# Agent attention with a squared-ReLU feed-forward layer: casting every high half by DMA, and squaring every fifth block on VectorE

## The chip, the cores and the metric

The kernel runs on one core of a Trainium2 chip. The metric is the device time of one execution in microseconds (us); the median over runs is compared.

## The reference, cut to what matters

```python
def sm(a, b):
    s = scale * (a @ b.transpose(0, 2, 1))
    e = np.exp(s - s.max(-1, keepdims=True))
    return e / (e.sum(-1, keepdims=True) + 1e-09)
agent_v = sm(agents, k) @ v          # 4 batches, 12480 keys, 49 agents, 128 channels
x = sm(q, agents) @ agent_v          # 4 x 12480 queries
h = x.reshape(49920, 128) @ w_in     # 128 x 2048
r = np.maximum(h, 0.0)
out = (r * r) @ w_out                # 2048 x 128
```

All inputs are float32.

## The kernel before, in words

**The work.** The 49920 tokens are cut into 52 groups of 960 (two halves of 480 columns), the 2048 hidden units into 16 slices of 128. A pair of group and slice is a block; blocks are numbered i = 0 to 831, 16 to a group. `agent_v @ w_in` is multiplied out once for a batch (`w_make`), so that a block begins with the softmax weights of its group (49 rows for each half, kept as `p_a` and `p_b`).

**Two-part numbers.** A matmul on rounded float32 (fp32r) loses the low bits. So each operand is split into a high half (a cast to fp32r) and a low half (the value minus the high one), and a product is made of three matmuls: high with high, high with low, low with high.

**A block's path.** `mm1` (L401): six matmuls into a PSUM tile h, of which there are two. `relu` (L413) and `square` (L417), both on ScalarE, write g. `high` (L420) casts g to gh: for even blocks, and for all of the first 48, by a DMA that GpSimd issues (L423); otherwise by a copy on VectorE (L425); the last four blocks always take VectorE. `low` (L427) subtracts on VectorE and gives gl. `mm2` (L431) makes twelve matmuls of a block, six for each half, that add up in a PSUM pair `out` over the 16 blocks of a group. The two row halves of TensorE work side by side on the two banks of the pair, and for each pair of blocks the banks change sides once; between the sides a nop on GpSimd (L442, the relay) must pass. There are 10 buffers of g, 9 of gh and 7 of gl.

**The order.** One list holds every step with a time in units of blocks; each engine does its steps in the order of these times. Block i has `mm1` at i, `relu` at i + 0.1, `square` at i + 1.2, `high` at i + 3.05 (DMA) or i + 2.35, `low` at i + 5.2 (DMA) or i + 4.3. `mm2` follows LAG = 8 steps behind: an even block j with j + 1, one side at step j + 8, the other at j + 9. The times order the engines' queues; when a step runs is decided by its waits.

**The output.** After a group's last `mm2` ScalarE copies one half of `out` to ob and VectorE the other (`store_a` L458, `store_d` L462), and SP stores ob (L477). SP also issues all loads of queries, keys and values (six buffers in all, shared) and the four small transfers of `q_spread` (L374), in one queue.

**The attention part** is put between the blocks by a planner (`chain`, L504), which gives each step of a chain of engines the first free place in the list and keeps the PSUM pair that the insertion uses free of others (`held`, L522): `plan_queries` (L538) for two groups at a time, `plan_keys` and `plan_bias` for the next batch's keys, `plan_values` for exp, the turn of the weights (`k_turn`, tile pe), `v_acc` and, at its end, `a_final` and four `w_make`. `q_hi` (L383) casts a group's softmax weights by a GpSimd DMA to `p_a`, `q_lo` (L387) makes `p_b` on VectorE. Before the first block the keys and values of batch 0 are worked through in an order written by hand (from L602).

Of the kernel before, what the change touches and what calls it, by code (L numbers as in the profile page):

```python
# [17 lines left out]
P = 128  # L18
# [9 lines left out]
def agent_attention_relu2_kernel(ctx: ExitStack, tc: tile.TileContext, qT, kT, v, agT, w_in, w_out, outT):  # L28
# [354 lines left out]
    def q_hi(s):  # L383
        PT[s] = (wk.tile([P, TT], F32R, name="p_a"), wk.tile([P, TT], F32R, name="p_b"))
        nc.gpsimd.dma_start(out=PT[s][0][:M], in_=pts[s][:M])

# [30 lines left out]
    def square(i):  # L417
        nc.scalar.activation(gs[i], gs[i], AF.Square)  # L418

# [10 lines left out]

    def mm2(i, turn, first=False, last=False):  # L431

        s, j = divmod(i, NF)
        gh, gl = ghs[i], gls[i]
        if first:
            group[0] = s
            o = pair(s, "out")
            outs[s] = [o[:, t] for t in range(2)]
        o = outs[s]
        relay = None  # L440
        if turn != seen["turn"] and not first:
            relay = nc.gpsimd.nop()  # L442
            tc.add_manual_dep(relay.ins, seen["mm"].ins.name, SYNC, reason="bank changes row tile")
        for n, (w, g) in enumerate(((wo_hi, gh), (wo_lo, gh), (wo_hi, gl))):
            for t, rows in enumerate((LOW, HIGH)):
                u = t ^ turn
                mm = nc.tensor.matmul(o[u][:, :TT], w[rows, j, :], two(g[rows, u, :]), start=first and n == 0, stop=last and n == 2)  # L447
# [3 lines left out]
        done[i] = done.get(i, 0) + 1  # L451
        if done[i] == 2:
            ghs.pop(i), gls.pop(i)

    done = {}
    obs = {}

    def store_a(s):  # L458
        nc.scalar.copy(ob_of(s)[:, 0, :], outs[s][0][:, :TT])  # L459
        store(s)  # L460

    def store_d(s):  # L462
        nc.vector.tensor_copy(ob_of(s)[:, 1, :], outs[s][1][:, :TT])  # L463
        store(s)

    def ob_of(s):
        if s not in obs:
            obs[s] = wk.tile([P, 2, TT], F32, name="ob", bufs=1)
        return obs[s]

    def store(s):
        stored[s] = stored.get(s, 0) + 1
        if stored[s] == 2:
            ob = obs.pop(s)
            outs.pop(s)
            if s < NSG - 1:
                nc.sync.dma_start(out=outT[:, s * ST:(s + 1) * ST], in_=ob.rearrange("p t n -> p (t n)"))  # L477
            else:
                for t in range(2):
                    nc.sync.dma_start(out=outT[:, s * ST + t * TT:s * ST + (t + 1) * TT], in_=ob[:, t, :])  # L480

    stored = {}

    LAG = 8
    TAIL = 36
    SKIP = (7, 12)
    FROM = 0

    def by_dma(i):
        return FROM <= i < NG - 4 and (i % 2 == 0 or i < 3 * NF)  # L490

    steps = []

    def at(t, f, *args):
# [43 lines left out]
    def plan_queries(u):  # L538

        first, t = chain(32 * u - 46, [("PE", q_scores, u), ("DVE", q_turn, u)])  # L540
        for x, s in enumerate(members(u)):
            at(first - LEAD + .1 * x, q_load, s)
        plan_rows(u, t + 2)

    def plan_rows(u, g):
        todo = [("DVE", q_max, u), ("DVE", q_sub, u), ("ACT", q_exp, u), ("DVE", q_total, u), ("DVE", q_norm, u), ("DVE", q_back, u)]
        for e, f, _ in todo:
            _, t = chain(g, [(e, f, u)])
            g = t + 2
        at(t + .9, q_spread, u)  # L550
        plan_halves(u, t + 6)

    def plan_halves(u, t):
        for s in members(u):
            _, t = chain(max(t, s * NF - 9 if s > 1 else 0), [("POOL", q_hi, s), ("DVE", q_lo, s)])
            assert t + 1 < s * NF, (s, t)

    def plan_keys(b, n, t):

        first, end = chain(t, [("PE", k_scores, b, n), ("ACT", k_copy, n), ("DVE", k_max, n)])  # L560
        for x in range(2):
            if b > 1 or n > 1:
                at(first - LEAD + .1 * x, k_load, b, 2 * n + x)
        return end

# [4 lines left out]
    def plan_values(b, t0, stop):  # L570

        used = {}
        d = (stop - TAIL - t0) / NP
        for n in range(NP):
            _, t1 = chain(max(t0 + 1 + int(n * d), used.get(n - 2, 0)), [("ACT", k_exp, n), ("DVE", k_turn, n)])
            used[n], end = chain(t1 + 3, [("PE", v_acc, n), ("DVE", v_sum, n)])
            for x in range(2):
                at(used[n] - LEAD + .1 * x, v_load, b, 2 * n + x)
            if b < B - 1:
                keys = plan_keys(b + 1, n, t1 + 6)  # L580
        last, end = chain(end + 2, [("PE", a_final, 0), ("DVE", a_final, 1), ("DVE", a_final, 2)])
        for f in range(F // 512):
            _, end = chain(max(end + 2, stop + 4 * f - 12), [("PE", w_make, b, f, 0), ("PX", w_make, b, f, 1), ("ACT", w_make, b, f, 2), ("DVE", w_make, b, f, 3)])
            assert end + 2 < stop + 4 * f, (b, f, end, stop)
        if b < B - 1:
            return max(last + 2, plan_bias(keys + 1))

# [76 lines left out]
    for n, t in ((0, (.6, .61, .62, 1.15, 1.2, 1.3)), (1, (3.2, 3.21, 3.3, 3.6, 3.7, 3.8)), (2, (9.1, 9.11, 9.3, 10.1, 10.3, 11.1)), (3, (12.1, 12.12, 12.3, 13.1, 13.3, 14.1))):  # L664
        convert(wo_make, n, [y - Z for y in t])
        at(t[5] + .1, wo_split, n, 0)
        at(t[5] + 2.1, wo_split, n, 1)
    for t in (1.45, 2.45, 4.45, 5.45):
# [9 lines left out]
    taken.update((("ACT", 5), ("DVE", 6), ("ACT", 7), ("DVE", 8)))  # L678
    plan_halves(1, 11)
    for f, t in ((2, 5), (3, 7)):  # L680
        for x, y in enumerate((.005, .02, .5, 1.4)):
            at(t + y, w_make, 0, f, x)
    for u in range(2, NSG // 2 + 1):
        plan_queries(u)
    end = 22
    for n in range(NP):
# [5 lines left out]
    for i in range(NG):  # L692
        late = i in SKIP or i < NF + LAG and (i < LAG or (i - LAG) % NF == 0)
        at(i if late else i + .01, mm1, i)
        at(i + .1, relu, i)
        at(i + 1.2, square, i)
        if by_dma(i):
            at(i + 3.05, high, i)
            at(i + 5.2, low, i)
        else:  # L700
            at(i + 2.35, high, i)
            at(i + 4.3, low, i)
    for i in range(NF + LAG):
        j = i - LAG + sum(i <= x for x in SKIP)
        if j >= 0 and i not in SKIP:
            for x in range(2):
                at(i + (.03 if x else .005 if j == 0 else 0), mm2, j, x ^ (j % 2), x == 0 and j == 0, x == 1 and j == NF - 1)
    for j in range(NF, NG - LAG, 2):
        for x in range(2):
            for y in range(2):  # L710
                at(j + LAG + x + .001 * y, mm2, j + y, x ^ (j // 2 % 2), x + y + j % NF == 0, x + y == 2 and j % NF == NF - 2)
    for s in range(NSG - 1):
        t = s * NF + NF - 1 + LAG
        at(t + (.003 if s else .031), store_a, s)
        at(t + (.004 if s else .032), store_d, s)
    t, way = NG, (NG - LAG) // 2 % 2
    for js in (range(NG - LAG, NG - LAG // 2), range(NG - LAG // 2, NG)):
        for x in range(2):
            for j in js:
                at(t, mm2, j, way ^ x, False, x == 1 and j == NG - 1)  # L720
                t += 1
        way ^= 1
    at(t + .1, store_a, NSG - 1)
    at(t + .2, store_d, NSG - 1)
    with tc.manual_schedule():
# [32 lines left out]
```

## Time and profile before

| | us |
|---|---|
| median of 3 runs | 1781.02 |
| lowest and highest run | 1777.61, 1786.03 |
| the profiled execution's own time | 1783.28 |
| its span, first to last instruction | 1781.5 |
| TensorE busy in it (matmul) | 1736.2 |
| ScalarE busy | 1606.2 |
| VectorE busy | 1457.4 |
| GpSimd busy | 283.7 |

The profile is of one execution on the chip. Busy time is the time in which an engine works on an instruction; waits, register work and the issuing of a DMA by SP are not counted. The ends of matmuls are modelled, so TensorE's busy time says little alone. A wait is put down to what came last by the profile.

### The profile page before, as it was taken

Reading aid. Unit: us, or ns where it says so; the run is one execution under the profiler, and the core shown is the slowest. Engines: PE = TensorE matmul, PEld = TensorE weight load, DVE = VectorE, ACT = ScalarE, POOL = GpSimd, SP = SyncE. Lnnn points to the kernel's source line nnn. Section 1 sums busy time; section 2 is a strip of 40 time slices with the busy share of each in tenths; the row PEclk is TensorE's granted clock in tenths of the full one; section 3 lists DMA queues with packets and bytes.
Section 4 is the critical chain, followed back from the end, with each engine's and each line's share of the span. In section 5 each row is a group of like instructions: output and inputs, shape, how many; then the busy total and the mean of one; then the engine's idle time right before and its main releaser. Section 6 shows DMA issues by size and latency. Waiting matters only on the chain.

```text
span 1781.5 us, 41424 instructions
## 1 busy us (share of the span) xinstructions
PE 1736.2 (97%) x16841; PEld 1496.3 (84%) x16841; DVE 1457.4 (82%) x1740; ACT 1606.2 (90%) x1853; POOL 283.7 (16%) x509
## 2 busy tenths in 40 slices
PE   7899999999999999999999999999999999999998
PEld 3577888887888889887888889888988988988898
DVE  5876888878878888977878978888886887888887
ACT  3688989998889999999899999999998999999997
POOL 0232111111111111111111111111111111111110
PEclk8999999999999999999999999999999999999999
DMA  9689566666456567467356455456545545555553
GB/s 369 234 302 343 185 208 229 201 229 201 151 177 196 183 213 239 142 215 234 130 177 224 149 199 193 158 190 204 168 159 161 181 159 186 182 166 172 172 172 111
DMA packets 113791, 350.13 MB, mean 197 GB/s; under 512 B 15628, under 2 KB 28416, under 8 KB 113600
## 3 DMA queue, kind: packets, MB, share of 16 engines
q0 software_dynamic: 71264, 227.90, 37.4%
q1 hardware_dynamic: 42336, 119.59, 21.0%
q8 instruction: 132, 2.16, 0.5%
q14 instruction: 59, 0.48, 0.1%
HBM read 81.47 MB, written 25.56 MB: 60 GB/s over the span
## 4 chain that ended last, share of the span: by engine, by line
PE 80%; DMA 9%; DVE 4%; issue 3%; ACT 3%; POOL 0%; POOLq 0%; DVEq 0%; ACTq 0%
PE out L447 48%; PE h L411 24%; DMA gh<-g 9%; PE ps_att L167 4%; PE ps_att L230 2%; DVE gl L429 2%; ACT g L418 2%; ACT g L415 1%; PE out L230 1%; PE ps_att L310 1%; PE out L597 0%; DMA p_a<-pt 0%; DMA pt<-et 0%; DVE mxs L185 0%; DVE gh L425 0%
## 5 line engine op out<-in xcount | busy, mean ns | idle before, releaser
L429 DVE TENSOR_TENSOR gl<-g,gh 128x960 fp32r<-128x960 f32 x832 | 922.6, 1148 | 139.4 <-DMA gh<-g 134.5
L415 ACT ACTIVATE g<-h 128x960 f32<-128x960 f32 x832 | 820.1, 986 | 125.2 <-PE h L411 124.6
L418 ACT ACTIVATE g<-g 128x960 f32<-128x960 f32 x832 | 845.6, 1016 | 0.0
L447 PE MATMUL out<-gh,wo_hi 64*128 64x480 f32 x3328 | 623.4, 371 | 5.3 <-POOLq L442 3.1
L447 PE MATMUL out<-gl,wo_hi 64*128 64x480 f32 x3328 | 613.3, 365 | 7.3 <-DVE gl L429 6.9
L447 PE MATMUL out<-gh,wo_lo 64*128 64x480 f32 x3328 | 609.4, 363 | 0.0
L423 POOL DMA_DIRECT2D gh<-g x438 | 245.2, 560 | 1404.8 <-ACT g L418 482.9
L447 PEld LDWEIGHTS out<-gh,wo_hi 64*128 64x128 f32 x3328 | 314.0, 185 | 72.9 <-issue 38.9
L447 PEld LDWEIGHTS out<-gl,wo_hi 64*128 64x128 f32 x3328 | 314.5, 186 | 42.2 <-DVE gl L429 18.5
L447 PEld LDWEIGHTS out<-gh,wo_lo 64*128 64x128 f32 x3328 | 317.2, 187 | 22.0
L411 PE MATMUL h<-p_a,w_a 49*128 49x480 f32 x1664 | 310.9, 370 | 0.4 <-ACT w_a L294 0.4
L411 PE MATMUL h<-p_b,w_a 49*128 49x480 f32 x1664 | 304.2, 362 | 1.0 <-DVE p_b L388 1.0
L411 PE MATMUL h<-p_a,w_b 49*128 49x480 f32 x1664 | 304.6, 363 | 0.0
L425 DVE CAST gh<-g 128x960 fp32r<-128x960 f32 x394 | 257.0, 652 | 3.1 <-ACT g L418 3.0
L411 PEld LDWEIGHTS h<-p_a,w_a 49*128 49x128 f32 x1664 | 158.3, 187 | 16.4 <-ACT g L415 1.4
L411 PEld LDWEIGHTS h<-p_b,w_a 49*128 49x128 f32 x1664 | 159.8, 189 | 12.5 <-DVE p_b L388 1.4
L411 PEld LDWEIGHTS h<-p_a,w_b 49*128 49x128 f32 x1664 | 156.4, 184 | 13.0
L463 DVE COPY ob<-out 128x480 f32<-128x480 f32 x52 | 34.2, 658 | 108.1 <-ACT ob L459 108.1
L344 DVE STREAM_TRANSPOSE e<-ps_att 128x960 f32<-128x960 f32 (+1 forms) x26 | 30.7, 1182 | 34.9 <-PE ps_att L167 34.9
L167 PE MATMUL ps_att<-qt,ag_sb 128*32 128x480 f32 x408 | 47.3, 572 | 0.0
L209 ACT ACTIVATE sk<-sk,mb 128x448 f32<-128x448 f32 x56 | 33.9, 665 | 8.6 <-DVE mb L205 8.6
L230 PE MATMUL ps_att<-vt,pe 128*49 128x129 f32 x588 | 36.7, 275 | 2.1 <-DVE mxs L185 1.6
(92 smaller groups left out, 624.9 us busy)
## 6 DMA issues: line engine op xcount, KB each, us to landing
gh<-g POOLq DMA_DIRECT2D x438, 480.0 KB, 3.2
vt<-v SPq DMA_DIRECT2D x56, 451.5 KB, 9.3
kt<-kT SPq DMA_DIRECT2D x56, 448.0 KB, 6.6
qt<-qT SPq DMA_DIRECT2D x52, 480.0 KB, 7.2
outT<-ob SPq DMA_DIRECT2D x51, 480.0 KB, 3.5
pt<-et SPq DMA_DIRECT2D x204, 60.0 KB, 2.4
p_a<-pt POOLq DMA_DIRECT2D x52, 211.9 KB, 3.5
raw<-w_in SPq DMA_DIRECT2D x4, 512.0 KB, 10.9
```

The lines of the kernel that those rows point to most:

```text
L167: nc.tensor.matmul(ps[32 * j:32 * j + 32, h, :w], ags[j // 2][:, 32 * h:32 * h + 32], xs[j // 2][:, j % 2 * w:j % 2 * w + w], start=True, ...
L209: nc.scalar.activation(sk[:, n, h], sk[:, n, h], AF.Exp, bias=mb[:, h:h + 1], scale=scale)
L230: nc.tensor.matmul(ps[t:t + A, :C + 1], pes[n][:, c, :A], vt[:, y, :], start=n == first and c < 2, stop=n == last and c >= KC - 2)
L344: nc.vector.transpose(squares(es[u]), pss.pop(("q", u))[r, :, :TT].rearrange("p h (b c) -> p h b c", c=32))
L411: nc.tensor.matmul(hs[i][:, t, :TT], w, two(p), start=n == 0, stop=n == 2)
L415: nc.scalar.activation(gs[i], hs.pop(i)[:, :, :TT], AF.Relu)
L418: nc.scalar.activation(gs[i], gs[i], AF.Square)
L423: nc.gpsimd.dma_start(out=ghs[i], in_=gs[i])
L425: nc.vector.tensor_copy(ghs[i], gs[i])
L429: nc.vector.tensor_tensor(out=gls[i], in0=gs.pop(i), in1=ghs[i].bitcast(F32), op=ALU.subtract)
L447: mm = nc.tensor.matmul(o[u][:, :TT], w[rows, j, :], two(g[rows, u, :]), start=first and n == 0, stop=last and n == 2)
L463: nc.vector.tensor_copy(ob_of(s)[:, 1, :], outs[s][1][:, :TT])
```

## The change

All high halves but those of the last four blocks are cast by DMA. From block 32 on every block with i % 5 == 3 is squared by VectorE. `mm2` takes two blocks (in the last eight steps four) in one call: first all matmuls on gh, then those on gl. The output of a group is copied by one VectorE operation (the last group's still by two engines). `low` stands at i + 5.3 or i + 5.9. The first two groups' `q_hi` is a copy on ScalarE, and at the start `q_hi` and `q_lo` of group 0 stand behind the third and fourth turn of pe. In the planner, insertions hold their pair for longer, query scores come up to 14 steps earlier, the `w_make` of later batches get fixed places before all else, and the keys of the next batch are planned after the values.

```diff
     def q_hi(s):
...
-        nc.gpsimd.dma_start(out=PT[s][0][:M], in_=pts[s][:M])
+        if s > 1:
+            nc.gpsimd.dma_start(out=PT[s][0][:M], in_=pts[s][:M])
+        else:
+            nc.scalar.copy(PT[s][0][:M], pts[s][:M])
...
     def square(i):
-        nc.scalar.activation(gs[i], gs[i], AF.Square)
+        if by_vector(i):
+            nc.vector.tensor_tensor(gs[i], gs[i], gs[i], op=ALU.mult)
+        else:
+            nc.scalar.activation(gs[i], gs[i], AF.Square)
...
-    def mm2(i, turn, first=False, last=False):
+    def mm2(js, turn, first=False, last=False):
...
-        for n, (w, g) in enumerate(((wo_hi, gh), (wo_lo, gh), (wo_hi, gl))):
+        todo = [(w, g[i], i % NF) for ws, g in (((wo_hi, wo_lo), ghs), ((wo_hi,), gls)) for i in js for w in ws]
+        for n, (w, g, j) in enumerate(todo):
...
-    def store_a(s):
-        nc.scalar.copy(ob_of(s)[:, 0, :], outs[s][0][:, :TT])
-        store(s)
-
-    def store_d(s):
-        nc.vector.tensor_copy(ob_of(s)[:, 1, :], outs[s][1][:, :TT])
-        store(s)
...
     def store(s):
+        ob = wk.tile([P, 2, TT], F32, name="ob", bufs=1)
+        o = outs.pop(s)
+        if s < NSG - 1:
+            nc.vector.tensor_copy(ob, o[:, :, :TT])
+            nc.sync.dma_start(out=outT[:, s * ST:(s + 1) * ST], in_=ob.rearrange("p t n -> p (t n)"))
...
     def by_dma(i):
-        return FROM <= i < NG - 4 and (i % 2 == 0 or i < 3 * NF)
+        return i < NG - 4
+
+    def by_vector(i):
+        return i >= 2 * NF and i % 5 == 3 and by_dma(i)
...
-    taken = {(e, s * NF + NF - 1 + LAG) for s in range(NSG) for e in ("ACT", "DVE")}
+    taken = {(e, s * NF + NF - 1 + LAG) for s in range(NSG) for e in ("DVE",)}
...
-                held = range(ts[0], ts[-1] + (3 if todo[0][1] is v_acc else 2)) if todo[0][0] == "PE" else ()
+                held = range(ts[0], ts[-1] + (4 if todo[0][1] is v_acc else 2 if todo[0][1] is w_make else 3)) if todo[0][0] == "PE" else ()
...
-        first, t = chain(32 * u - 46, [("PE", q_scores, u), ("DVE", q_turn, u)])
+        first, t = chain(max(18, 32 * u - 60), [("PE", q_scores, u), ("DVE", q_turn, u)])
...
-            if b < B - 1:
-                keys = plan_keys(b + 1, n, t1 + 6)
...
-        for f in range(F // 512):
-            _, end = chain(max(end + 2, stop + 4 * f - 12), [("PE", w_make, b, f, 0), ("PX", w_make, b, f, 1), ("ACT", w_make, b, f, 2), ("DVE", w_make, b, f, 3)])
...
         if b < B - 1:
+            for n in range(NP):
+                keys = plan_keys(b + 1, n, turned[n][1] + 5)
...
-    for f, y in ((q_turn, .05), (q_max, .8), (q_sub, .81), (q_exp, 2.4), (q_total, 3.9), (q_norm, 4.8), (q_back, 5.4), (q_hi, 11), (q_lo, 17)):
+    for f, y in ((q_turn, .05), (q_max, .8), (q_sub, .81), (q_exp, 2.4), (q_total, 3.9), (q_norm, 4.8), (q_back, 5.4), (q_hi, order["t", 2] + 1 - t), (q_lo, order["t", 3] + 1 - t)):
...
+    for b in range(1, B):
+        for f, x in enumerate((-6, -3, 0, 4)):
+            first, end = chain(b * NS * NF + x, [("PE", w_make, b, f, 0), ("PX", w_make, b, f, 1), ("ACT", w_make, b, f, 2), ("DVE", w_make, b, f, 3)])
...
-            at(i + 5.2, low, i)
+            at(i + (5.3 if i % 2 else 5.9), low, i)
...
     for s in range(NSG - 1):
         t = s * NF + NF - 1 + LAG
-        at(t + (.003 if s else .031), store_a, s)
-        at(t + (.004 if s else .032), store_d, s)
+        at(t + .6, store, s)
```

## Rows read from the trace of the kernel before

**Rows 1.** The page: busy time (share of span) and instructions by engine; DMA in all.

```profile
PE 1736.2 (97%) x16841; PEld 1496.3 (84%) x16841; DVE 1457.4 (82%) x1740; ACT 1606.2 (90%) x1853; POOL 283.7 (16%) x509
...
DMA packets 113791, 350.13 MB, mean 197 GB/s; under 512 B 15628, under 2 KB 28416, under 8 KB 113600
```

**Rows 2.** Stretches: length, busy time of PE, PEld, DVE, ACT, POOL, clock, DMA share, GB/s.

```profile
1618.50:1650.00 31.50, 31.50 (x310) 27.82 (x308) 28.27 (x35) 29.59 (x35) 5.19 (x9) 1.00 0.43 149
1650.00:1678.90 28.90, 28.90 (x288) 26.88 (x286) 24.39 (x29) 28.90 (x34) 4.89 (x9) 1.00 0.61 196
```

**Rows 3.** Waits of TensorE's matmuls, 150 us to the end: total, times, longest (us).

```profile
PE ps_att L310 <- DVE w_b L321: 6.7, 3, 2.9
PE out L447 <- DVE gl L429: 6.7, 21, 0.5
PE ps_att L261 <- DVE mxs L185: 4.0, 2, 2.5
PE out L447 <- DMA gh<-g: 1.8, 3, 0.8
PE ps_att L230 <- DVE mxs L185: 1.6, 1, 1.6
```

**Rows 4.** Waits of VectorE over the whole span.

```profile
DVE gl L429 <- DMA gh<-g: 134.5, 75, 4.5
...
DVE ob L463 <- ACT ob L459: 108.1, 52, 4.1
```

**Rows 5.** Chain of waits, 400 to 520 us: start, length (us), what.

```profile
428.96 8.86 DMA gh<-g
...
440.64 1.01 DVE mxs L185
```

**Rows 6.** The page's groups: count | busy, mean ns of one | idle before, releaser.

```profile
L429 DVE TENSOR_TENSOR gl<-g,gh 128x960 fp32r<-128x960 f32 x832 | 922.6, 1148 | 139.4 <-DMA gh<-g 134.5
...
L418 ACT ACTIVATE g<-g 128x960 f32<-128x960 f32 x832 | 845.6, 1016 | 0.0
...
L423 POOL DMA_DIRECT2D gh<-g x438 | 245.2, 560 | 1404.8 <-ACT g L418 482.9
...
L411 PE MATMUL h<-p_b,w_a 49*128 49x480 f32 x1664 | 304.2, 362 | 1.0 <-DVE p_b L388 1.0
...
L425 DVE CAST gh<-g 128x960 fp32r<-128x960 f32 x394 | 257.0, 652 | 3.1 <-ACT g L418 3.0
...
L463 DVE COPY ob<-out 128x480 f32<-128x480 f32 x52 | 34.2, 658 | 108.1 <-ACT ob L459 108.1
L344 DVE STREAM_TRANSPOSE e<-ps_att 128x960 f32<-128x960 f32 (+1 forms) x26 | 30.7, 1182 | 34.9 <-PE ps_att L167 34.9
```

**Rows 7.** The stretch of 100 to 170 us, columns as in rows 2.

```profile
100.00:170.00 70.00, 69.53 (x666) 55.36 (x664) 47.20 (x48) 61.75 (x71) 18.70 (x36) 1.00 0.95 320
```

**Rows 8.** DMA issues in that stretch: count, size, median us from issue to landing.

```profile
gh<-g POOLq DMA_DIRECT2D x33, 480.0 KB, 6.5
```

**Rows 9.** Waits of TensorE's matmuls in that stretch, all of them.

```profile
PE out L447 <- DVE gl L429: 0.3, 1, 0.3
```

**Rows 10.** Timeline of VectorE and TensorE at the start: start, length, [idle before <-releaser].

```profile
33.06 0.66 DVE L388 TENSOR_TENSOR p_b<-pt,p_a 113x480 fp32r<-113x480 f32 x1 [5.47 <-DMA p_a<-pt]
...
36.31 13.21 PE L230 MATMUL out<-vt,pe 128*49 128x129 f32 x196 [5.49 <-DVE pe L213]
```

**Rows 11.** The vt loads before 50 us: duration ns, first and last start us; landing.

```profile
L219 SPq DMA_DIRECT2D vt<-v x14: 327/328/328, 15.2 to 34.5; - x14
...
DMA to landing us min/median/max: 9.1/10.3/13.3
```

**Rows 12.** L423, the gh transfers issued from 1026 to 1046 us.

```profile
DMA to landing us min/median/max: 2.8/5.7/9.1
```

**Rows 13.** Waits of TensorE's weight loads for the halves, 1020 to 1050 us.

```profile
PEld out L447 <- DVE gl L429: 1.5, 2, 0.9
PEld out L447 <- DMA gh<-g: 1.2, 1, 1.2
```

More of the change, by code (lines that the diff above doesn't have):

```diff
@@ L429, in low @@
         nc.vector.tensor_tensor(out=gls[i], in0=gs.pop(i), in1=ghs[i].bitcast(F32), op=ALU.subtract)
-    def mm2(i, turn, first=False, last=False):
-        s, j = divmod(i, NF)
-        gh, gl = ghs[i], gls[i]
+    def mm2(js, turn, first=False, last=False):
+        s = js[0] // NF
         if first:
@@ L437, in mm2 @@
             o = pair(s, "out")
-            outs[s] = [o[:, t] for t in range(2)]
+            outs[s] = o
         o = outs[s]
@@ L443, in mm2 @@
             tc.add_manual_dep(relay.ins, seen["mm"].ins.name, SYNC, reason="bank changes row tile")
-        for n, (w, g) in enumerate(((wo_hi, gh), (wo_lo, gh), (wo_hi, gl))):
+        todo = [(w, g[i], i % NF) for ws, g in (((wo_hi, wo_lo), ghs), ((wo_hi,), gls)) for i in js for w in ws]
+        for n, (w, g, j) in enumerate(todo):
             for t, rows in enumerate((LOW, HIGH)):
                 u = t ^ turn
-                mm = nc.tensor.matmul(o[u][:, :TT], w[rows, j, :], two(g[rows, u, :]), start=first and n == 0, stop=last and n == 2)
+                mm = nc.tensor.matmul(o[:, u, :TT], w[rows, j, :], two(g[rows, u, :]), start=first and n == 0, stop=last and n == len(todo) - 1)
                 if relay is not None:
@@ L450, in mm2 @@
         seen.update(mm=mm, turn=turn)
-        done[i] = done.get(i, 0) + 1
-        if done[i] == 2:
-            ghs.pop(i), gls.pop(i)
+        for i in js:
+            done[i] = done.get(i, 0) + 1
+            if done[i] == 2:
+                ghs.pop(i), gls.pop(i)
     done = {}
     obs = {}
-    def store_a(s):
-        nc.scalar.copy(ob_of(s)[:, 0, :], outs[s][0][:, :TT])
-        store(s)
-    def store_d(s):
-        nc.vector.tensor_copy(ob_of(s)[:, 1, :], outs[s][1][:, :TT])
-        store(s)
[L466 to L469, printed above, removed]
-    def store(s):
[L472 to L482, printed above, removed]
+    def store(s):
+        ob = wk.tile([P, 2, TT], F32, name="ob", bufs=1)
[3 more added lines that the diff above has]
+            nc.sync.dma_start(out=outT[:, s * ST:(s + 1) * ST], in_=ob.rearrange("p t n -> p (t n)"))
+        else:
+            nc.scalar.copy(ob[:, 0, :], o[:, 0, :TT])
+            nc.vector.tensor_copy(ob[:, 1, :], o[:, 1, :TT])
+            for t in range(2):
+                nc.sync.dma_start(out=outT[:, s * ST + t * TT:s * ST + (t + 1) * TT], in_=ob[:, t, :])
     LAG = 8
@@ L486, in agent_attention_relu2_kernel @@
     SKIP = (7, 12)
-    FROM = 0
     def by_dma(i):
-        return FROM <= i < NG - 4 and (i % 2 == 0 or i < 3 * NF)
+        return i < NG - 4
+    def by_vector(i):
+        return i >= 2 * NF and i % 5 == 3 and by_dma(i)
     steps = []
@@ L538, in plan_queries, with plan_rows @@
     def plan_queries(u):
-        first, t = chain(32 * u - 46, [("PE", q_scores, u), ("DVE", q_turn, u)])
+        first, t = chain(max(18, 32 * u - 60), [("PE", q_scores, u), ("DVE", q_turn, u)])
         for x, s in enumerate(members(u)):
             at(first - LEAD + .1 * x, q_load, s)
-        plan_rows(u, t + 2)
-    def plan_rows(u, g):
+        plan_rows(u, t + 2, 32 * u - 37)
+    def plan_rows(u, g, free):
         todo = [("DVE", q_max, u), ("DVE", q_sub, u), ("ACT", q_exp, u), ("DVE", q_total, u), ("DVE", q_norm, u), ("DVE", q_back, u)]
@@ L548, in plan_rows @@
             _, t = chain(g, [(e, f, u)])
-            g = t + 2
+            g = t + (3 if u > 2 else 2)
+        t = max(t, free)
         at(t + .9, q_spread, u)
@@ L554, in plan_halves @@
         for s in members(u):
-            _, t = chain(max(t, s * NF - 9 if s > 1 else 0), [("POOL", q_hi, s), ("DVE", q_lo, s)])
+            _, t = chain(max(t, s * NF - 9 if s > 1 else 0), [("POOL" if s > 1 else "ACT", q_hi, s), ("DVE", q_lo, s)])
             assert t + 1 < s * NF, (s, t)
@@ L563, in plan_keys @@
                 at(first - LEAD + .1 * x, k_load, b, 2 * n + x)
+        print('K', b, n, first, end)
         return end
@@ L570, in plan_values @@
     def plan_values(b, t0, stop):
-        used = {}
+        used, turned = {}, {}
         d = (stop - TAIL - t0) / NP
         for n in range(NP):
-            _, t1 = chain(max(t0 + 1 + int(n * d), used.get(n - 2, 0)), [("ACT", k_exp, n), ("DVE", k_turn, n)])
+            _, t1 = turned[n] = chain(max(t0 + 1 + int(n * d), used.get(n - 2, 0)), [("ACT", k_exp, n), ("DVE", k_turn, n)])
+            print('V', b, n, t1)
             used[n], end = chain(t1 + 3, [("PE", v_acc, n), ("DVE", v_sum, n)])
@@ L578, in plan_values @@
                 at(used[n] - LEAD + .1 * x, v_load, b, 2 * n + x)
-            if b < B - 1:
-                keys = plan_keys(b + 1, n, t1 + 6)
+        print('Vend', b, end, stop)
         last, end = chain(end + 2, [("PE", a_final, 0), ("DVE", a_final, 1), ("DVE", a_final, 2)])
-        for f in range(F // 512):
-            _, end = chain(max(end + 2, stop + 4 * f - 12), [("PE", w_make, b, f, 0), ("PX", w_make, b, f, 1), ("ACT", w_make, b, f, 2), ("DVE", w_make, b, f, 3)])
-            assert end + 2 < stop + 4 * f, (b, f, end, stop)
+        assert end < stop - 6, (b, end, stop)
         if b < B - 1:
+            for n in range(NP):
+                keys = plan_keys(b + 1, n, turned[n][1] + 5)
             return max(last + 2, plan_bias(keys + 1))
@@ L665, in agent_attention_relu2_kernel @@
         convert(wo_make, n, [y - Z for y in t])
-        at(t[5] + .1, wo_split, n, 0)
-        at(t[5] + 2.1, wo_split, n, 1)
+        at(t[5] + .8, wo_split, n, 0)
+        at(t[5] + 3, wo_split, n, 1)
     for t in (1.45, 2.45, 4.45, 5.45):
@@ L678, in agent_attention_relu2_kernel @@
     taken.update((("ACT", 5), ("DVE", 6), ("ACT", 7), ("DVE", 8)))
-    plan_halves(1, 11)
-    for f, t in ((2, 5), (3, 7)):
+    plan_halves(1, 13)
+    for f, t in ((2, 1.6), (3, 7)):
         for x, y in enumerate((.005, .02, .5, 1.4)):
             at(t + y, w_make, 0, f, x)
+    for b in range(1, B):
+        for f, x in enumerate((-6, -3, 0, 4)):
+            first, end = chain(b * NS * NF + x, [("PE", w_make, b, f, 0), ("PX", w_make, b, f, 1), ("ACT", w_make, b, f, 2), ("DVE", w_make, b, f, 3)])
+            assert x >= 4 * f - 12 and end < b * NS * NF + min(4 * f, LAG), (b, f, first, end)
     for u in range(2, NSG // 2 + 1):
         plan_queries(u)
-    end = 22
+    end = 19
     for n in range(NP):
@@ L695, in agent_attention_relu2_kernel @@
         at(i + .1, relu, i)
-        at(i + 1.2, square, i)
+        at(i + (1.3 if by_vector(i) else 1.2), square, i)
         if by_dma(i):
             at(i + 3.05, high, i)
-            at(i + 5.2, low, i)
+            at(i + (5.3 if i % 2 else 5.9), low, i)
         else:
@@ L706, in agent_attention_relu2_kernel @@
             for x in range(2):
-                at(i + (.03 if x else .005 if j == 0 else 0), mm2, j, x ^ (j % 2), x == 0 and j == 0, x == 1 and j == NF - 1)
+                at(i + (.03 if x else .005 if j == 0 else 0), mm2, (j,), x ^ (j % 2), x == 0 and j == 0, x == 1 and j == NF - 1)
     for j in range(NF, NG - LAG, 2):
         for x in range(2):
-            for y in range(2):
-                at(j + LAG + x + .001 * y, mm2, j + y, x ^ (j // 2 % 2), x + y + j % NF == 0, x + y == 2 and j % NF == NF - 2)
+            at(j + LAG + x, mm2, (j, j + 1), x ^ (j // 2 % 2), x + j % NF == 0, x == 1 and j % NF == NF - 2)
     for s in range(NSG - 1):
         t = s * NF + NF - 1 + LAG
-        at(t + (.003 if s else .031), store_a, s)
-        at(t + (.004 if s else .032), store_d, s)
+        at(t + .6, store, s)
     t, way = NG, (NG - LAG) // 2 % 2
@@ L718, in agent_attention_relu2_kernel @@
         for x in range(2):
-            for j in js:
-                at(t, mm2, j, way ^ x, False, x == 1 and j == NG - 1)
-                t += 1
+            t += 1
+            at(t, mm2, js, way ^ x, False, x == 1 and NG - 1 in js)
+        t += 1
         way ^= 1
-    at(t + .1, store_a, NSG - 1)
-    at(t + .2, store_d, NSG - 1)
+    at(t + .1, store, NSG - 1)
     with tc.manual_schedule():
```

## The prediction

> **What bounds the kernel now.** I read the busy times first: TensorE is busy for 1736.2 of 1781.5 us, ScalarE for 1606.2, VectorE for 1457.4 [rows 1]. Since a modelled matmul can look busy while it waits, the second view is two groups of 16 blocks in the table of stretches: with nothing inserted 16 blocks take 28.9 us, with one insertion of query scores 31.5 us [rows 2]. In the first ScalarE is busy for all 28.9 us, and so is TensorE; both are at their floor there. 52 groups at 28.9 us are 1503 us, and the matmuls of the attention part must be added to that. The change takes away no matmul, so only waiting of TensorE can be won, and a relieved ScalarE wins nothing by itself. The third view is who TensorE waits for after the first 150 us: in total 20.8 us [rows 3], 8.5 us of it for the low and high halves of the activations (gl, gh), 12.3 us at insertions (w_make, a_final, v_acc) for a VectorE operation that frees or fills their bank.
>
> Both kinds have one root. VectorE takes its work in order, and it stood 134.5 us waiting for the DMA that casts gh and 108.1 us for ScalarE's half of the output copy [rows 4]. With 1457.4 us busy these two make 1700 us: VectorE has little left to catch up with. The chain of waits shows it: a gh transfer of 8.86 us, and 3 us after its landing the maximum (mxs) that a_final's bank waited for [rows 5].
>
> **The change, part by part.** The sum is made against the profiled execution's own 1783.3 us, which is 2.3 us above the median of the runs.
>
> (1) *Casts to DMA.* 390 of 394 casts leave VectorE: 390 x 0.652 = 254 us [rows 6]. Each becomes a DMA issue on GpSimd of 0.560 us [rows 6], 218 us more on an engine that is busy 283.7 us [rows 1]; nothing but the relay of mm2 (the nop that passes a bank between row tiles) stands behind them.
>
> (2) *Squares.* Blocks 33, 38, ... 823, 159 of them, go to VectorE. The nearest row is the low half, the same operation and shape: 159 x 1.148 = 183 us [rows 6] onto VectorE, 159 x 1.016 = 162 us off ScalarE. Their DMA issue now waits for VectorE, and what is queued behind it on GpSimd is the relay that TensorE needs two blocks at a time; a late VectorE can stop TensorE by that way too. Price: nothing while VectorE is on time (below: nothing excludes a small gain; above: see the third rival).
>
> (3) *Output.* 51 copies of 480 columns from PSUM (0.658 us) become copies of 960. No such copy is in the trace; the transpose of 960 columns from PSUM takes 1.182 us [rows 6], two halves would be 1.316 us, and one half is the other end. I take 1.18, nearest in shape: 51 x 0.52 = 27 us more on VectorE. ScalarE loses its copy, and with it the 108.1 us of waiting go. The SP queue's store, with the loads behind it, waits for one copy instead of two engines; I price that at nothing.
>
> VectorE in sum: 1457 - 254 + 183 + 27 = 1413 us busy, and 108 us less waiting. It gains some 150 us of slack over the span, under 3 us per group.
>
> (4) *Order.* mm2 takes two blocks in one call and the low halves last; the same matmuls, the low half of an even block is needed two weight steps later, and the low halves stand 0.1 to 1.0 step later in VectorE's order, so a late transfer holds VectorE for less. Query scores come 14 steps earlier with their two loads of 480 KB and, later, their four small transfers on SP; w_make gets fixed places, keys come after values. No instruction is added, and every one runs under TensorE's work if its bank is free. What it can win are the 12.3 us at insertions: I take 9, the ends are 0 and 12.3, nearer to the upper because two things that held VectorE (ScalarE's copy and the early place of the low half) are eased.
>
> (5) *Waits for gl and gh after 150 us.* The stretch from 100 to 170 us already sends all high halves by DMA, moves 320 GB/s [rows 7], and gh lands after 6.5 us in the median [rows 8]; TensorE waits there for 0.3 us [rows 9]. The whole run after the change moves 350 MB [rows 1] and 390 x 0.4915 = 192 MB more, 542 MB, which over 1765 us is 307 GB/s, a little less than in that stretch. At 0.3 us per 70 us the remaining 1630 us would cost 7 us in place of 8.5: I take -1.5. The ends are -8.5 and the price of the second rival.
>
> (6) *Start.* VectorE waits 5.47 us for the DMA that makes p_a, and only then turns the first pe tile; TensorE's 13.21 us of v_acc start at 36.31 us for that reason [rows 10]. With the high half copied by ScalarE and the subtraction placed behind the fourth turn, v_acc could start some 5.5 us earlier. What is late next is the data: the last vt load is issued at 34.5 us and lands 9.1 us later at the earliest [rows 11], so v_acc ends near 44.5 instead of 49.5 us. I take -5.0; the ends are 0 and -5.5. The same edit for the second group takes away the 1.0 us that TensorE waited for p_b [rows 6]: -1.0.
>
> Sum: -9 - 1.5 - 5 - 1 = -16.5 us, so 1766.8 us for an execution like the profiled one, and with the 2.3 us between it and the median **1765 us**.
>
> **A rule against a row.** A single gh transfer lands after 2.8 us at best, and after 9.1 us when issued just behind an output store with the loads that the store had held back [rows 12]. So the other queue took far more than half. The Trainium skill's page "DMA: Bandwidth & Descriptors", in "Queues, rings and completion order", says that an engine goes round between the queue rows it has work for, a packet at a time. By that rule gh would get half and land within 5.6 us; the sum would be that of the first rival. This trace does not agree with it.
>
> **The rivals.**
>
> *First: transfers never late.* If a gh transfer beside loads took at most twice 2.8 us, TensorE would wait for no half and VectorE would hold no bank: all 20.8 us go, with the start 26.8. 1783.3 - 26.8 - 2.3 = 1754 us. Against it stand the 8.86 and 9.1 us [rows 5, 12]; for it, that VectorE's slack may do the same.
>
> *Second, the other side: the late transfer decides.* Query loads come in pairs once in 32 blocks, 26 times. In one such burst TensorE's weight loads waited 2.7 us for gh and gl [rows 13]. Until now only even blocks depended on the DMA there; an odd block's low half is due one step (1.81 us) sooner after its issue. If three bursts of four cost 2.7 us (20 x 2.7 = 54 us in place of the 20.8), the time is 1783.3 - 6 - 20.8 + 54 - 2.3 = 1808 us. It decides from the point where gh of odd blocks lands later than about 8 us while no insertion stretches the step. For it: twice as many transfers meet each burst. Against it: the 0.3 us in the stretch where it was already so [rows 9], though VectorE had more slack there.
>
> *Third: given back.* VectorE, late after each burst, squares late; its DMA issue blocks GpSimd, and the relay stops TensorE. Half of the 159 squares are of odd blocks, whose issue stands just in front of a relay: 80 x 0.16 us = 13 us would return nearly all of the gain, 1778 us. For it: ScalarE, which squared on time, is replaced by an engine that does not have the time to spare. Against it: no relay is among TensorE's waits after 150 us [rows 3].
>
> **How the numbers follow.** Forecast 0.46, first rival 0.13, second 0.20, third 0.21. A measurement of this kernel can tell about 0.5% (8.9 us) from no change, so faster is below 1772, slower above 1790. Faster: 0.41 of the forecast and the first rival, 0.54. Same: 0.05 of the forecast and 0.19 of the third, 0.24. Slower: the second and 0.02 of the third, 0.22. The range runs from 1748 (the first rival, a few us below for the upper ends of (4) and (6)) to 1802, which leaves out the worse half of the second rival and a little of the first.
>
> **What would show it.** Right: v_acc starts near 31 us; VectorE's wait for ScalarE's output copy is gone; casts are x4, squares on VectorE x159 at about 1.15 us; TensorE's waits after 150 us add up to 10 us or less; a group without insertions still takes 28.9 us; the DMA moves some 307 GB/s. Wrong: gh landing at a median over 6 us through the whole run, and TensorE waiting for gl or gh by 40 us or more (second rival); or waits of TensorE for the GpSimd relay (third). The forecast would also fall if groups without insertions grew longer, since I price all of this change as waits.

## The result: 1.4% slower

| | before | after |
|---|---|---|
| median of four runs, us | 1780.34 | 1806.16 |
| lowest and highest run | 1777.61, 1786.03 | 1799.76, 1812.47 |
| the profiled execution, its span | 1783.28, 1781.5 | 1806.67, 1804.9 |

The ratio is 1.0141, with a 95% interval of 1.0097 to 1.0184. The forecast (1765 us, range 1748 to 1802) fell; the second rival (1808 us) has the sign and, as shown below, the mechanism; that its number comes so close is in part luck.

**The profile after.** From the page: busy times, DMA total, the two queues that carry the data, and the chain by engine.

```profile
PE 1748.7 (97%) x16831; PEld 1493.8 (83%) x16835; DVE 1449.7 (80%) x1509; ACT 1471.4 (82%) x1645; POOL 477.7 (26%) x897
...
DMA packets 169664, 541.42 MB, mean 300 GB/s; under 512 B 21806, under 2 KB 34368, under 8 KB 169472
...
q0 software_dynamic: 127136, 419.18, 68.7%
q1 hardware_dynamic: 42336, 119.59, 21.3%
...
PE 68%; DMA 17%; issue 6%; DVE 4%; ACT 3%; POOL 0%; SPq 0%; POOLq 0%; DVEq 0%; ACTq 0%
```

Beside [rows 1]: ScalarE lost 135 us of work, GpSimd gained 194, VectorE is where it was. The DMA moves 541 MB, as worked out, and 17% of the chain that ended last is now DMA. The groups of instructions, from the page (answering to [rows 6]):

```profile
L435 DVE TENSOR_TENSOR gl<-g,gh 128x960 fp32r<-128x960 f32 x832 | 934.3, 1149 | 242.1 <-DMA gh<-g 208.8
L418 ACT ACTIVATE g<-h 128x960 f32<-128x960 f32 x832 | 807.7, 971 | 286.2 <-PE h L414 282.9
L429 POOL DMA_DIRECT2D gh<-g x828 | 439.5, 531 | 1243.3 <-ACT g L424 724.5
...
L422 DVE TENSOR_TENSOR g<-g 128x960 f32<-128x960 f32 x159 | 183.0, 1151 | 29.2 <-ACT g L418 28.2
```

The last column is the idle time just before each group. VectorE's wait for gh rose from 134.5 us [rows 4] to 208.8, and ScalarE now waits 282.9 us for TensorE: the relieved engine only waits. The waits that set the time are those of TensorE after 150 us (total, times, longest; answering to [rows 3]):

```profile
PE out L453 <- DMA gh<-g: 16.7, 19, 2.5
PE out L453 <- DVE gl L435: 12.6, 34, 0.6
PE out L453 <- POOLq L447: 5.6, 12, 0.5
```

A matmul's end is modelled, so some waiting hides under matmuls. The waits of TensorE's weight loads show more of it. First after the change, then before it, both after 150 us, waits put down to "issue" left out:

```profile
PEld out L453 <- DVE gl L435: 31.8, 56, 0.9
PEld out L453 <- DMA gh<-g: 27.4, 31, 2.8
PEld out L453 <- POOLq L447: 12.4, 19, 0.9
```

```profile
PEld out L447 <- DVE gl L429: 17.9, 31, 0.9
PEld ps_att L310 <- DVE w_b L321: 7.8, 3, 3.3
...
PEld ps_att L261 <- DVE mxs L185: 4.8, 2, 2.9
PEld out L447 <- DMA gh<-g: 3.1, 4, 1.2
PEld ps_att L230 <- DVE mxs L185: 2.0, 1, 2.0
PEld ps_att L230 <- DVE pe L213: 1.2, 2, 0.9
PEld out L447 <- POOLq L442: 1.0, 2, 0.5
```

The change did what it was to do at the insertions: 15.8 us of waiting (w_b, mxs, pe) are gone. But the waits for the two halves went from 21.0 to 59.2 us, and the relay's from 1.0 to 12.4. One such wait in the chain (start, us, what):

```profile
1014.13 9.76 DMA gh<-g
...
1024.01 1.17 DVE gl L435
...
1025.22 0.77 PE out L453
```

A high half takes 9.76 us to land, the low half follows, and only then does TensorE go on. Counted over all gh transfers after 200 us, 12 of 384 took over 8 us to land before, and 83 of 764 after.

What makes them late is seen when they are sorted by how many of SP's large transfers (loads and output stores of 448 to 480 KB) were in flight at their issue. Of the 764, 489 had none: they landed after 3.7 us in the median, and 3 of them took over 8 us. Of the 81 that had three or more, 57 took over 8 us, and the median is 8.5 us (before the change 12 of 55, and 7.4 us). A rival can be left aside here: more traffic did not make the engines' own large operations slower. A low half takes 1.149 us after and 1.148 before [rows 6].

What TensorE's clock did behind the wait that ends at 1024 us is seen in stretches of 2 us (columns as in [rows 2]; the third number from the right is the granted clock):

```profile
1022.00:1024.00 2.00, 0.07 (x2) 0.07 (x2) 0.00 (x0) 1.11 (x2) 0.00 (x0) 1.00 1.14 409
1024.00:1026.00 2.00, 1.60 (x10) 1.13 (x12) 1.99 (x2) 0.00 (x0) 0.00 (x0) 0.67 0.60 217
1026.00:1028.00 2.00, 2.00 (x12) 1.50 (x12) 2.00 (x3) 0.77 (x1) 1.06 (x2) 0.50 0.12 40
1028.00:1030.00 2.00, 2.00 (x12) 1.67 (x12) 2.00 (x3) 1.09 (x2) 0.53 (x1) 0.50 1.04 329
1030.00:1032.00 2.00, 2.00 (x14) 1.70 (x14) 2.00 (x3) 1.17 (x2) 0.00 (x0) 0.63 1.09 328
1032.00:1034.00 2.00, 2.00 (x32) 1.65 (x30) 0.56 (x1) 1.63 (x3) 0.53 (x1) 1.00 0.80 235
```

TensorE stands nearly still for 2 us, then runs at the lower level (0.50, that is 1.2 of 2.4 GHz) until about 1031 us: 12 matmuls in 2 us, where a group without insertions runs 288 in 29.2 us, 20 in 2 us. Summed over such stretches from 150 us to the last matmul, 2 us times what is missing to a granted clock of 1, the clock cost 10.2 us in four places after, and 6.8 us in three places before.

The balance of the two spans: the halves +38.2, the relay +11.4, the insertions -15.8, the clock +3.4, the start -7.2 (the first `relu` begins 4.0 us earlier, and group 0 takes 3.2 us less). That is +30.0 where the spans differ by +23.4; the rest was not followed further (a weight load can wait while earlier matmuls still run, so its waits may count too much).

### The profile page after: what moved, and what is told of

Same layout as the page of the kernel before. It is cut to its first block, busy times and chain, and to the rows that moved or that the text cites. A ratio compares the mean times of both kernels' runs of the same rounds, so it can differ in the third digit from the quotient of the medians.

```text
span 1804.9 us, 41518 instructions
## 1 busy us (share of the span) xinstructions
PE 1748.7 (97%) x16831; PEld 1493.8 (83%) x16835; DVE 1449.7 (80%) x1509; ACT 1471.4 (82%) x1645; POOL 477.7 (26%) x897
## 4 chain that ended last, share of the span: by engine, by line
PE 68%; DMA 17%; issue 6%; DVE 4%; ACT 3%; POOL 0%; SPq 0%; POOLq 0%; DVEq 0%; ACTq 0%
PE out L453 41%; PE h L414 20%; DMA gh<-g 16%; PE ps_att L167 4%; ACT g L424 3%; DVE gl L435 3%; PE ps_att L230 1%; DMA kt<-kT 1%; PE ps_att L310 1%; PE out L230 0%; ACT g L418 0%; DVE g L422 0%; DVE cv_x L88 0%; POOL wo_lo L113 0%; PE h L167 0%
## 5 line engine op out<-in xcount | busy, mean ns | idle before, releaser
L435 DVE TENSOR_TENSOR gl<-g,gh 128x960 fp32r<-128x960 f32 x832 | 934.3, 1149 | 242.1 <-DMA gh<-g 208.8
L418 ACT ACTIVATE g<-h 128x960 f32<-128x960 f32 x832 | 807.7, 971 | 286.2 <-PE h L414 282.9
L429 POOL DMA_DIRECT2D gh<-g x828 | 439.5, 531 | 1243.3 <-ACT g L424 724.5
L424 ACT ACTIVATE g<-g 128x960 f32<-128x960 f32 x673 | 670.7, 997 | 0.0
L453 PE MATMUL out<-gl,wo_hi 64*128 64x480 f32 x3328 | 490.8, 368 | 15.7 <-DVE gl L435 15.2
L422 DVE TENSOR_TENSOR g<-g 128x960 f32<-128x960 f32 x159 | 183.0, 1151 | 29.2 <-ACT g L418 28.2
L469 DVE COPY ob<-out 128x960 f32<-128x960 f32 x51 | 58.7, 1151 | 14.5 <-PE out L453 14.2
L344 DVE STREAM_TRANSPOSE e<-ps_att 128x960 f32<-128x960 f32 (+1 forms) x26 | 30.7, 1179 | 10.8 <-PE ps_att L167 10.5
L230 PEld LDWEIGHTS ps_att<-vt,pe 128*49 128x49 f32 x588 | 31.4, 123 | 6.4 <-issue 5.2
```

The source lines that it names most:

```text
L230: nc.tensor.matmul(ps[t:t + A, :C + 1], pes[n][:, c, :A], vt[:, y, :], start=n == first and c < 2, stop=n == last and c >= KC - 2)
L344: nc.vector.transpose(squares(es[u]), pss.pop(("q", u))[r, :, :TT].rearrange("p h (b c) -> p h b c", c=32))
L418: nc.scalar.activation(gs[i], hs.pop(i)[:, :, :TT], AF.Relu)
L422: nc.vector.tensor_tensor(gs[i], gs[i], gs[i], op=ALU.mult)
L429: nc.gpsimd.dma_start(out=ghs[i], in_=gs[i])
L435: nc.vector.tensor_tensor(out=gls[i], in0=gs.pop(i), in1=ghs[i].bitcast(F32), op=ALU.subtract)
```

## The experiments

Three theories were on trial. *Late transfers* (first): high halves that land late beside SP's loads stop TensorE. *Late squares* (second): VectorE squares late, its DMA issue blocks GpSimd, and the relay stops TensorE. *Load* (third): the mean traffic of the DMA is what counts, however it is spread. Ratios are to the kernel before, timed on the same chip. Edits are made to the kernel after unless said otherwise.

**e1: the old division of work, in the new order.** Odd blocks are cast by VectorE again, all squares are on ScalarE, and the low halves have their old place.

```diff
-        return i < NG - 4
+        return i < NG - 4 and (i % 2 == 0 or i < 3 * NF)
...
-        return i >= 2 * NF and i % 5 == 3 and by_dma(i)
+        return False
...
-            at(i + (5.3 if i % 2 else 5.9), low, i)
+            at(i + 5.2, low, i)
```

> The kernel after with the old division of the work (odd blocks from 48 on cast on VectorE, all squares on ScalarE, low at i + 5.2); the new places, the merged mm2 and the single output copy stay. Theory 1 (late transfers: twice as many gh transfers land too late when the loads that an output store held back run beside them): the waits for gh and gl go back to those of before or below, the insertion waits stay gone, the start stays 4 us earlier: 1755 to 1772 us. Theory 2 (late squares on VectorE block GpSimd and its relay): the same fall, 1755 to 1772. If the new places themselves cost time, it stays above 1780.

Measured: 1743.02 us, ratio 0.977 (0.9747 to 0.9794). It beats both kernels. TensorE's waits after 150 us:

```profile
PE out L453 <- DVE gl L435: 2.3, 5, 0.6
PE ps_att L310 <- DVE w_b L321: 0.7, 1, 0.7
PE ps_att L230 <- DVE pe L213: 0.2, 1, 0.2
```

7 of 382 transfers after 200 us take over 8 us, and the granted clock does not fall once between 150 us and the last 2 us. ScalarE is busier than after (1594.9 us) and it costs nothing. So places, merged `mm2`, output copy and start are worth 39 us together, and the division of work, with the place of the low halves that belongs to it, takes away 63.

**e2: no squares on VectorE.**

```diff
-        return i >= 2 * NF and i % 5 == 3 and by_dma(i)
+        return False
```

> The kernel after with every square on ScalarE. Theory 1: the transfers are what they were, so the time stays at 1800 to 1812 us and gh still lands at 8 to 10 us in each burst. Theory 2: the time falls to 1785 us or less, and the relay waits of TensorE go.

Measured: 1805.41 us, ratio 1.0137 (1.0096 to 1.0178), the same as after.

```profile
PE out L453 <- DMA gh<-g: 23.3, 23, 2.4
PE out L453 <- DVE gl L435: 12.1, 31, 0.6
PE out L453 <- POOLq L447: 0.3, 1, 0.3
```

The relay's waits go (5.6 to 0.3) and the time stays: the waits for gh take their place. The mechanism of late squares is real, but it sets nothing; that theory falls. It falls by the time; the profiled execution took 1817.44 us, 12 us more than the median, so its waits are not those of a median one.

**e3: the kernel before, with all casts by DMA.** Nothing else is changed.

```diff
-        return FROM <= i < NG - 4 and (i % 2 == 0 or i < 3 * NF)
+        return i < NG - 4
```

> The kernel before with one edit: every high half but the last four by DMA. VectorE is relieved of 254 us. Theory 1: slower than before all the same, 1800 to 1825 us, with TensorE waiting over 30 us for gh and gl. Theory 2: no slower than before, 1770 to 1783 us, as the squares stay on ScalarE.

Measured: 1818.88 us, ratio 1.0188 (1.0156 to 1.0221).

```profile
PE out L447 <- DVE gl L429: 23.1, 44, 1.0
PE out L447 <- DMA gh<-g: 13.4, 17, 1.7
```

The casts alone make the kernel before 37 us slower, in the old order too, though VectorE is busy for 1262.5 us, 195 less. Its slack does not shield TensorE from a late transfer.

**e4: the output stored from ScalarE's queue.** SP's loads no longer queue behind a store that waits for its copy; the bytes are the same.

```diff
-            nc.sync.dma_start(out=outT[:, s * ST:(s + 1) * ST], in_=ob.rearrange("p t n -> p (t n)"))
+            nc.scalar.dma_start(out=outT[:, s * ST:(s + 1) * ST], in_=ob.rearrange("p t n -> p (t n)"))
```

> The kernel after with the output store issued from ScalarE's queue, so that the loads on SP are no longer held back and set free in a burst. Theory 1: the loads spread out, gh lands later than 8 us more rarely, and 10 to 25 us come back: 1780 to 1796 us. Theory 2: 1800 to 1812 us. Theory 3 (the DMA engines are simply full, 90% on average, bursts or not): 1800 to 1812 us, with the median landing unchanged at 4.7 us.

Measured: 1781.35 us, ratio 0.9992 (0.9975 to 1.0008), so 25 us less than after.

```profile
PE out L453 <- DVE gl L435: 9.3, 24, 0.6
PE out L453 <- DMA gh<-g: 8.6, 10, 2.3
PE out L453 <- POOLq L447: 2.5, 6, 0.7
```

51 transfers take over 8 us in place of 83, 61 are issued with three or more large transfers in flight in place of 81, and the clock holds at 1 from 150 us to the last matmul. The same traffic, only spread otherwise, gives back 25 of the 63 us, so mean load alone is not the cause. It is not all bunching either: 38 us to e1 are left.

**e5: the kernel before with the single output copy by VectorE.**

```diff
-            outs[s] = [o[:, t] for t in range(2)]
+            outs[s] = o
...
-    at(t + .1, store_a, NSG - 1)
-    at(t + .2, store_d, NSG - 1)
+    at(t + .1, store, NSG - 1)
```

> The kernel before with one part of the change: the output of a group copied by one VectorE operation, in the old place. If VectorE's 108 us of waiting for ScalarE's copy is what made the insertions wait, most of the gain of the old division with the new places shows here: 1755 to 1770 us. If the new places make the gain, it stays at 1776 to 1783 us.

Measured: 1771.83 us, ratio 0.9928 (0.9906 to 0.9951). This lies between the two that were expected. The 108.1 us [rows 4] go and 12.7 us of time with them, but in the profiled execution (1778.01 us) the insertions still wait (4.6 for w_b, 4.5 and 1.7 for mxs). My step (4) supposed that easing VectorE would cure those, and here it did not; in the new order most of them go even with the old copy (e9).

**e6: e1 and e4 together.** The store's edit of e4 on top of the three of e1.

```diff
-            nc.sync.dma_start(out=outT[:, s * ST:(s + 1) * ST], in_=ob.rearrange("p t n -> p (t n)"))
+            nc.scalar.dma_start(out=outT[:, s * ST:(s + 1) * ST], in_=ob.rearrange("p t n -> p (t n)"))
...
-        return i < NG - 4
+        return i < NG - 4 and (i % 2 == 0 or i < 3 * NF)
```

> The old division in the new places, with the store on ScalarE's queue as well. If bursts of loads behind the store still cost something with 438 gh transfers, 1735 to 1741 us; if TensorE has nothing left to wait for (2.3 us after 150 us), 1740 to 1746 us: the same.

Measured: 1767.77 us, ratio 0.99 (0.9874 to 0.9926): over 1% slower than e1 (0.977), where I expected no loss. First TensorE's longest wait, then the wait of ScalarE that stands behind it:

```profile
PE h L414 <- ACT g L418: 12.2, 19, 1.7
...
ACT g L418 <- DVE ob L469: 34.1, 20, 2.7
```

The store's issue waits on ScalarE for VectorE's copy, and the next `relu` waits behind it. In e4 ScalarE had time for that (1465.8 us busy), here it has none. An edit that helps a kernel with late transfers hurts the one without them.

**e7: three quarters of the blocks by DMA** (633 transfers, no squares on VectorE).

```diff
-        return i < NG - 4
+        return i < NG - 4 and (i % 4 != 1 or i < 3 * NF)
...
-        return i >= 2 * NF and i % 5 == 3 and by_dma(i)
+        return False
```

> The kernel after with every square on ScalarE and of the odd blocks every second one cast on VectorE: 633 gh transfers in place of 828 or 438. Theory 1 (lateness grows with the number of transfers that meet a burst): between the two, 1760 to 1785 us, TensorE waiting some 10 to 20 us for gh and gl after 150 us. Theory 3 (the mean load of the DMA engines is the bound, 90% before it): as fast as with 438, 1740 to 1750 us, since the load falls to about 75%.

Measured: 1775.01 us, ratio 0.9944 (0.9922 to 0.9966).

```profile
PE out L453 <- DMA gh<-g: 8.2, 8, 2.2
PE out L453 <- DVE gl L435: 7.8, 20, 0.6
```

438, 633 and 828 transfers give ratios of 0.977, 0.9944 and 1.0137 (e1, e7, e2): 31 us for the first 195 transfers, 34 us for the next 195, with no threshold seen between these three. That is what theory 1 expected of e7 and not what theory 3 did.

**e8: e1 with the odd blocks by DMA in place of the even ones.** The number is the same, but an odd block's half is due one step sooner. (The low halves keep the place that they have after the change, for an odd block 0.1 step behind that of e1.)

```diff
-        return i < NG - 4
+        return i < NG - 4 and (i % 2 == 1 or i < 3 * NF)
...
-        return i >= 2 * NF and i % 5 == 3 and by_dma(i)
+        return False
```

> As many transfers as in the old division (438), but the odd blocks by DMA and the even ones on VectorE, squares on ScalarE. If the shorter way of an odd block (its low half is due one step sooner) decides, 1755 to 1785 us and TensorE waits 10 us or more for gh and gl; if only the number of transfers decides, 1740 to 1748 us.

Measured: 1752.27 us, ratio 0.9816 (0.9794 to 0.9837), outside what was expected of either side. Against the two runs of e1 (0.977 and 0.9787) the shorter way of the odd blocks costs 0.3 to 0.5%, 5 to 8 us of the 63 (the interval overlaps with that of the second); the number of transfers is the larger part.

**e9: e1 with the old two-engine output copy.**

```diff
+    def store_a(s):
+        nc.scalar.copy(ob_of(s)[:, 0, :], outs[s][:, 0, :TT])
+        store(s)
+
+    def store_d(s):
+        nc.vector.tensor_copy(ob_of(s)[:, 1, :], outs[s][:, 1, :TT])
+        store(s)
...
-        at(t + .6, store, s)
+        at(t + (.003 if s else .031), store_a, s)
+        at(t + (.004 if s else .032), store_d, s)
```

> The old division in the new places (1743 us), but with the output copied by two engines as before. It tells what the new places, the merged mm2 and the new start give without the single copy. If the places alone make the insertions free, 1745 to 1752 us; if they need VectorE's 108 us, TensorE's insertion waits come back and it is 1755 to 1768 us.

Measured: 1755.77 us, ratio 0.985 (0.9818 to 0.9882). VectorE waits 79.1 us for ScalarE's half again, and of TensorE's waits at insertions 3.6 us are left (2.0 for pe, 1.6 for w_b). So the time lies where the second expectation had it, but not for its reason: what came back is mostly waiting for the low and high halves, 13.3 us on the weight loads beside 3.6 in e1 again. Against e1 on the same chip (below) the single copy is worth 11.6 us.

**e10: e1 with the old start.** `q_hi` of group 0 by DMA, at its old place; group 1 as in e1.

```diff
-        if s > 1:
+        if s != 1:
...
-    for f, y in ((q_turn, .05), (q_max, .8), (q_sub, .81), (q_exp, 2.4), (q_total, 3.9), (q_norm, 4.8), (q_back, 5.4), (q_hi, order["t", 2] + 1 - t), (q_lo, order["t", 3] + 1 - t)):
+    for f, y in ((q_turn, .05), (q_max, .8), (q_sub, .81), (q_exp, 2.4), (q_total, 3.9), (q_norm, 4.8), (q_back, 5.4), (q_hi, 11), (q_lo, 17)):
```

> The old division in the new places (1743 us), but with q_hi of group 0 cast by DMA and q_hi and q_lo in their old places at the start. Step (6) of the prediction gave 5.0 us for this edit: 1748 us, with v_acc starting near 36 us again.

Measured: 1749.58 us, ratio 0.9819 (0.9779 to 0.9858), 5.4 us above e1. The start of v_acc, here and then in the kernel after (start, us, what; idle time before it):

```profile
36.48 3.90 PE L230 MATMUL out<-vt,pe 128*49 128x129 f32 x34 [5.82 <-DVE pe L213]
```

```profile
33.44 6.62 PE L230 MATMUL out<-vt,pe 128*49 128x129 f32 x112 [1.32 <-DVE pe L213]
```

The old wait of [rows 10] is back with the old order.

**e1 again,** the same kernel, on the chip of e9 and e10.

> The old division in the new places once more, beside the other two: 1740 to 1746 us.

Measured: 1744.16 us, ratio 0.9787 (0.9757 to 0.9816).

## Why the prediction was wrong

**(5), the waits for gl and gh: the step that failed.** I took -1.5 us, from 0.3 us of waiting in the stretch of 100 to 170 us [rows 7, 9], multiplied over the run. Measured it was +20.8 us on the matmuls, in which I had priced it (8.5 to 29.3), and +38.2 us on the weight loads. That stretch after the change:

```profile
100.00:170.00 70.00, 69.74 (x671) 55.97 (x670) 57.13 (x59) 60.26 (x67) 18.27 (x35) 1.00 1.01 340
```

No wait of TensorE's matmuls falls into it after the change either, at 340 GB/s, though 7 of its 32 high halves took over 8 us to land, the longest 9.7. They were no less late there than elsewhere; they had more time. It was a wrong sample, and [rows 7, 8] had said so: 33 transfers in 70 us are 2.1 us a block, since keys and values are inserted there, where a group without insertions takes 1.83. Counted in the trace after the change, the first matmul that reads a high half starts 9.0 us (odd blocks) and 10.5 us (even blocks) after its issue in that stretch, and 8.1 and 9.7 us over the run (medians). I compared GB/s and left out the pace; my text of the second rival had the condition ("while no insertion stretches the step") and I did not hold it against the stretch.

**The second rival** had the mechanism, and its limit of about 8 us is the 8.1 us that odd blocks have. That late transfers do it is shown by e1 and e7 (the number), e4 (the spreading, at equal bytes) and e3 (the casts alone, in the old kernel). Its 1808 us beside the measured 1806 are in part luck. The sum took away 20.8 us of waits on matmuls and put in 54 us of waits on weight loads (59.2 measured). With the 36.8 us that weight loads waited before (21.0 and 15.8) it gives 1792 us; the relay's 11.4 us and the clock's 3.4 us, which it did not have, fill the gap. Nor did its signs all come: gh lands after 4.7 us in the median, not over 6, and the waits for the halves pass 40 us on the weight loads alone. Its reason, that odd blocks are due sooner, explains only the 5 to 8 us of e8. How the rest divides between bunching and number is not settled: e4 gives 25 us for the one, but it moves ScalarE's queue too.

**The first rival** stood on the rule that two queues share an engine packet by packet. The six high halves issued from 1011.6 to 1019.6 us landed after 4.4 to 9.8 us, with a median of 8.2. The forecast rejected the rule by the landing time of one transfer as a whole; the last section shows that it fails in one part of that transfer and holds in the other. And having rejected it, the forecast drew too little from that.

**The third rival**'s wait came (the relay, 12.4 us on the weight loads), without its effect, as e2 shows. Its 0.16 us for each square of an odd block stood in no row; the 19 waits take 0.65 us each.

**(1) and (2)** cost the engines what was worked out: 828 issues at 0.531 us, 159 squares at 1.151 us. VectorE's busy time is 1449.7 us, where my sum was 1413, and yet none of its large operations got longer. Operations that follow each other overlap in the trace, and busy time counts the overlap once: the 832 low halves of [rows 6] make 955 us by their mean and 922.6 by busy time. All of VectorE's durations add up to 1572.9 us before and 1528.9 after, the 44 us less of my sum; the overlap fell from 115.4 to 79.2 us. So a sum of means says too much of what an engine is relieved of, in e3 too (195 us where 254 were taken).

**(3)** The copy of 960 columns takes 1.151 us (1.18 taken) and the wait of 108.1 us is gone. I counted this as slack and gave it no time of its own; it is worth 11.6 (e9) to 12.7 us (e5). **(4)** The waits at insertions are gone, 12.3 us where I took 9.

**(6)** The edit for group 0 gives 5.4 us (e10) where I took 5.0, but not as I saw it: v_acc starts at 33.4 us, not near 31. The wait of 5.47 us [rows 10] is gone, but the maximum (mxs) that comes before the turns was 2.6 us later in this trace (27.90 beside 25.27 us).

Measured from the first matmul of a group to that of the next, the 288 matmuls of a group without insertions or waits take 29.2 us before (from 1648.9 us) and after (from 1731.5 us); the 28.9 us of [rows 2] come from where that stretch begins and ends. So the change is in waits, as I priced it, and in the clock behind them. The parts that I priced right, or too low, carry e1's 39 us; some 12 of these are the copy and 5 the start, and no run parts the new places from the merged `mm2`. The one step that I mis-sized, with the relay and the clock behind it, takes 63.

## What to carry to other kernels

An operation that moves from an engine to the DMA gets a latency that depends on what else is queued: look at its worst landings and at the slack in the tightest stretch, not at its median nor at GB/s. A rate of waiting taken from one stretch holds for others only at the same pace. And relieving an engine that only shares the floor with TensorE wins nothing: here the best kernel, 2.1 to 2.3% under the one before, is the change without its headline part. No run issued the casts earlier or let `mm2` follow later, so whether more lead would have made the DMA casts pay is open.

## What was not expected of the hardware

**Beside loads, a software queue can move next to nothing for 4 us and then get nearly half.** Queues (q1 is SP's, q0 GpSimd's; packets, MB, busy share of the 16 engines) and issues (count, KB, median us to landing), before the change, from 1031.9 to 1036.2 us, around the transfer of 9.1 us [rows 12]:

```profile
q1 hardware_dynamic: 330, 1.15, 96.9%
q0 software_dynamic: 14, 0.02, 2.1%
...
gh<-g POOLq DMA_DIRECT2D x2, 480.0 KB, 8.5
```

From 1036.5 to 1041.5 us, up to just behind its landing:

```profile
q1 hardware_dynamic: 330, 1.05, 56.3%
q0 software_dynamic: 257, 0.92, 49.3%
```

After the change, from 1014.1 to 1019.9 us, around the transfer of 9.76 us:

```profile
q1 hardware_dynamic: 351, 1.18, 63.9%
q0 software_dynamic: 168, 0.55, 38.8%
...
gh<-g POOLq DMA_DIRECT2D x4, 480.0 KB, 8.8
```

With several loads of SP in flight GpSimd's queue got 2% of the engines for 4 us and nearly half for the next 5; after the change it got less than SP's, with four high halves in it. The Trainium skill's page "DMA: Bandwidth & Descriptors", in "Queues, rings and completion order", has an engine go round between the queues that have work, one packet at a time. The trace agrees in the second stretch (257 packets beside 330) and not in the first (14 beside 330), unless the packets of gh were not ready to be moved in those 4 us, which the trace does not show.

**A late operand can cost twice.** Three of the four places after the change where the granted clock falls lie behind a single wait of TensorE of 1.6 to 2.5 us for gh (the fourth behind 1.3 us of short ones), and for some 3 to 7 us the matmuls then run at 1.2 GHz. It is 10.2 us here, 6.8 before, and none in the traces of e1 and e4 between 150 us and the last matmul. Not every such wait does it: in e4 TensorE waits 2.3 us for gh before 814.1 us, and the granted clock stays at 1.00 behind it. My sum had no term for it.
